# MoBA attention and a GELU MLP on one core: another ending for the last output tile, another gate in front of the weight loads, and a new order

## The chip, the cores and the metric

The kernel runs on one core of a Trainium2 chip. The metric is the device time of one execution in microseconds (us). Eleven runs of the kernel before gave a median of 259.63 us, from 258.48 to 269.83. The core's engines are called as in the profile: PE (matmuls; PEld is its weight load), DVE (vector), ACT (scalar), POOL (gpsimd), and SP, which does nothing here but issue DMAs.

## The reference

Four batches (B), eight heads, 768 tokens (S), head size 64. Attention is causal and block-sparse: a token sees its own block of 64 and the three blocks whose mean key scores highest with its query. Its output, 3072 tokens by 512, goes through an MLP with 2048 hidden units. Inputs and outputs are float32.

```python
k_rep = k.reshape(B, H, n_blocks, block, D).mean(axis=3)
gate_scores = np.einsum('bhsd,bhnd->bhsn', q, k_rep)     # causal blocks only
top_idx = np.argsort(gate_scores, axis=-1)[..., -top_k:] # 3 blocks, and the own one
scores = scale * np.matmul(q, k.transpose(0, 1, 3, 2))   # masked, causal
attn = softmax(scores); x = attn @ v                     # x: [3072, 512]
h = x @ w_in
g = 0.5 * h * (1.0 + np.tanh(c * (h + 0.044715 * h * h * h)))
out = g @ w_out
```

## The kernel before

**Work.** Heads are taken in 16 pairs `p`, four to a batch. `load` (L406) brings one of k, q, v of a pair from HBM with DMAs on SP: two for the plain form, four (one per half head and head) for the form that DVE then turns with a 32x32 stream transpose (L585). `pre` (L549) makes keys and queries with the head dimension on partitions, the block means, the gate and the selection (DVE, L709 to L730). `heads2` (batch 0, L847) and `heads` (batches 1 to 3, L1028) do scores (PE, L866 and L1049), exp (ACT, L885 and L1062), the causal triangle (POOL, L911 and L1076) and the product with v (PE, L934 and L1088). `s1` (L1114) is the first MLP product, 128 matmuls of 384 columns per batch (L1124) with the GELU on ACT (L1136) into `G`. `s2_plain` (L1200) is the second MLP product of batch 0, 96 matmuls of 512 columns (L1206). `s2` (L1241) does it for batches 1 to 3 with Strassen's scheme in Winograd's form: seven products of half size instead of eight. `sums` and `w_sums` make the factors on DVE (L1194, L1176).

**The Strassen tile.** `token(t)` (L1244) treats 128 rows of the upper half and 128 of the lower half of a batch together. `half(m, side, h, ...)` (L1248) is product `m`: eight matmuls of 256 columns (L1254) into one half `h` of a PSUM bank called `side`. Products run on PE strictly in the order of the calls, since each waits for `prev`. The order is 1, 5 (bank P), 2, 6 (bank Q), 3, 4 (P again), 7 (Q again). DVE or ACT copies product 1 to the output tile `osb` (`ao`), and DVE adds the rest in joins (L1298): `eo` makes product 5 + product 1, `bo`, `co` and `do` each add 512 columns. Product 3 waits for `eo`, and product 7 for `bo`, because they go on top of a bank that these joins read. After `co` and after `do` SP stores 128 rows of 512 float32 (256 KB each, L1331).

**Weights.** `load_w` (L476) issues a weight matrix in two parts of 1024 KB (as float16) on POOL's DMA queue. In front of the first part stands a small POOL copy (L482) that reads 16 numbers of a loaded tile, so that POOL does not issue the load before that tile has landed. For `w_in` the tile is that of v of pair 3; for `w_out` it is that of q of pair 4, of which the copy reads partition 0, which the first of its four DMAs writes. `hold` (L490) is a tiny DMA on SP that reads the first part of a weight; the loads behind it on SP wait until that part has landed: k and q of pair 4 stand behind `w_in`, v of pair 4 and everything later behind `w_out`.

**Order.** Everything is one list of `Op`s with dependencies, engine costs and a priority. `Plan.solve` (L200) is a list scheduler: at each step it takes, of the operations that could start first on their engines, the one with the lowest priority number. It works with the written costs (`{PE: 0.2215}`, `{"DMA": 6.0}`, `lag`), and its DMA resource is one first-come queue. The priorities are `RANK` (L21), 1881 numbers, one for each operation in the order of its creation. Each engine then runs its instructions in the order that came out, each waiting by semaphores for what it really needs. The numbers of `RANK` are thus the only thing that sets the order within an engine.

**Fillers.** `warm` (L1346) makes 72 matmuls of the identity (L1351) of the lowest priority. The scheduler puts one wherever it sees PE without other work. What is left over at the end runs after the last product, while the last store is on its way.

Of the kernel before, what the change touches and what calls it, by code (L numbers as in the profile page):

```python
# [21 lines left out]
    165, 130, 222, 240, 129, 241, 103, 211, 111, 84, 211, 61, 51, 212, 293,  # L22
    65, 212, 231, 42, 284, 32, 3, 284, 39, 4, 283, 49, 650, 1, 285, 121, 29,
    285, 71, 30, 284, 48, 394, 18, 286, 90, 26, 286, 110, 139, 285, 158,
    368, 138, 286, 60, 355, 28, 642, 624, 324, 73, 519, 522, 326, 105, 352,
    72, 99, 67, 1018, 377, 83, 496, 380, 82, 107, 24, 36, 76, 164, 162, 56,
    373, 91, 85, 81, 13, 89, 168, 86, 34, 190, 1029, 449, 971, 156, 102,
    100, 52, 381, 346, 75, 429, 416, 117, 118, 621, 313, 114, 113, 827, 298,
    514, 261, 178, 186, 384, 273, 188, 479, 361, 309, 134, 534, 271, 209,
    199, 396, 424, 198, 392, 189, 136, 115, 575, 214, 109, 140, 453, 142,  # L30
    756, 141, 494, 120, 639, 174, 232, 295, 233, 15, 163, 557, 35, 58, 557,
    43, 351, 300, 428, 300, 19, 171, 135, 148, 239, 315, 254, 101, 108, 526,
    378, 362, 314, 206, 490, 182, 552, 379, 180, 296, 451, 312, 512, 345,
    289, 548, 311, 169, 393, 318, 194, 74, 170, 365, 316, 339, 181, 172,
    383, 317, 395, 237, 63, 504, 319, 275, 382, 260, 729, 247, 290, 421,
    288, 643, 272, 353, 277, 281, 55, 448, 246, 320, 347, 524, 610, 208,
    195, 244, 503, 616, 521, 226, 310, 336, 1098, 390, 341, 364, 333, 573,
    155, 269, 299, 358, 323, 482, 527, 553, 321, 488, 425, 253, 200, 335,
    350, 363, 297, 294, 680, 1271, 1270, 388, 54, 98, 322, 668, 264, 343,
    78, 325, 203, 95, 359, 354, 786, 357, 789, 520, 434, 509, 342, 467, 437,  # L40
    790, 389, 93, 782, 435, 44, 334, 258, 469, 80, 565, 344, 399, 77, 413,
    837, 414, 94, 41, 557, 251, 259, 149, 774, 776, 775, 797, 582, 64, 1439,
    1003, 550, 933, 934, 794, 11, 38, 125, 502, 505, 619, 1019, 529, 66,
    263, 577, 431, 433, 709, 221, 474, 498, 407, 412, 470, 397, 452, 436,
    473, 307, 947, 608, 723, 1233, 147, 1332, 1342, 945, 1313, 625, 948,
    843, 841, 928, 144, 736, 759, 611, 765, 478, 764, 713, 766, 936, 438,
    688, 955, 670, 737, 724, 653, 967, 1034, 1442, 252, 654, 1090, 607, 833,
    193, 951, 862, 950, 1310, 532, 823, 769, 1275, 1013, 97, 493, 1111, 536,
    444, 992, 531, 644, 618, 578, 215, 712, 663, 767, 783, 822, 1016, 798,
    1267, 924, 1491, 1512, 1408, 1407, 689, 844, 1216, 8, 213, 1200, 958,  # L50
    838, 940, 1091, 944, 969, 792, 793, 282, 265, 242, 305, 587, 651, 655,
    507, 419, 561, 703, 705, 728, 640, 959, 960, 785, 1070, 1184, 1182,
    1249, 201, 204, 205, 248, 262, 104, 249, 677, 686, 697, 719, 707, 661,
    750, 385, 386, 622, 540, 544, 546, 492, 614, 491, 338, 374, 268, 303,
    515, 517, 617, 612, 631, 635, 641, 460, 443, 463, 462, 458, 456, 555,
    687, 1017, 835, 1187, 267, 500, 143, 202, 183, 176, 349, 450, 486, 487,
    735, 747, 748, 1163, 1160, 1541, 572, 483, 1208, 440, 441, 484, 331,
    411, 806, 814, 706, 191, 497, 511, 855, 585, 468, 648, 851, 746, 623,
    613, 1062, 14, 235, 600, 682, 1064, 784, 132, 153, 1183, 849, 131, 700,
    666, 229, 696, 306, 791, 404, 472, 558, 45, 695, 558, 23, 606, 558, 53,  # L60
    694, 228, 37, 57, 40, 423, 238, 420, 699, 308, 541, 398, 400, 1066, 12,
    79, 250, 157, 197, 123, 658, 681, 207, 154, 725, 704, 702, 243, 768,
    543, 302, 664, 173, 757, 698, 701, 236, 669, 376, 678, 96, 636, 568,
    372, 406, 518, 586, 538, 192, 559, 27, 391, 559, 33, 216, 559, 47, 758,
    22, 21, 882, 150, 223, 220, 224, 665, 369, 913, 909, 230, 660, 124, 270,
    62, 175, 601, 119, 234, 405, 567, 50, 445, 551, 615, 432, 861, 638, 69,
    489, 889, 799, 426, 632, 566, 159, 459, 634, 562, 278, 554, 570, 1068,
    605, 749, 480, 917, 304, 560, 46, 161, 560, 31, 255, 560, 25, 225, 196,
    122, 771, 772, 166, 184, 167, 513, 218, 337, 872, 874, 633, 70, 564,
    177, 301, 455, 563, 466, 684, 457, 1079, 576, 753, 446, 811, 464, 942,  # L70
    584, 754, 877, 1734, 348, 581, 807, 910, 447, 943, 1311, 179, 360, 371,
    692, 547, 744, 340, 593, 592, 387, 595, 1540, 780, 185, 755, 859, 580,
    495, 481, 740, 287, 367, 210, 579, 596, 628, 589, 501, 442, 1222, 1225,
    1304, 824, 817, 809, 921, 1026, 925, 603, 927, 962, 1377, 961, 996, 781,
    1086, 1320, 923, 868, 860, 926, 691, 1354, 330, 329, 773, 1110, 1143,
    994, 998, 1317, 717, 734, 821, 836, 1380, 1083, 1085, 1103, 1134, 1256,
    597, 796, 667, 718, 1274, 328, 332, 733, 815, 953, 898, 869, 974, 1294,
    1132, 883, 919, 1159, 1539, 1228, 1231, 1567, 952, 1072, 1157, 939,
    1234, 1232, 499, 409, 410, 731, 832, 972, 1717, 1105, 1106, 1578, 1643,
    1664, 1683, 732, 770, 1658, 1728, 1727, 1648, 1645, 1253, 1735, 1492,  # L80
    803, 1287, 1358, 1494, 1631, 1646, 1603, 1661, 1653, 858, 1640, 1715,
    1718, 1714, 886, 187, 356, 16, 1639, 847, 1171, 716, 714, 863, 675, 676,
    829, 867, 1028, 1048, 1080, 893, 894, 891, 887, 941, 761, 1047, 1137,
    1056, 1206, 1331, 1333, 1336, 1052, 762, 1381, 1379, 1378, 1454, 1099,
    1337, 620, 5, 1375, 935, 984, 1081, 1084, 1089, 1189, 1082, 1154, 1053,
    1168, 599, 1076, 476, 475, 528, 604, 477, 1051, 1421, 1322, 1343, 1374,
    970, 1403, 1361, 1447, 1071, 1515, 1520, 1365, 1584, 1104, 116, 227, 20,
    133, 890, 1738, 127, 890, 1742, 92, 890, 1749, 465, 375, 68, 146, 145,
    1009, 1069, 523, 598, 1015, 1199, 506, 1197, 657, 739, 1224, 471, 266,
    1308, 1542, 1186, 1156, 918, 1535, 1528, 916, 1245, 1627, 1666, 826,  # L90
    1142, 1329, 760, 1152, 1012, 1366, 1607, 1153, 530, 1041, 1543, 1282,
    549, 973, 1513, 831, 1219, 880, 978, 1357, 1000, 106, 892, 1741, 257,
    892, 1736, 126, 892, 1737, 788, 590, 370, 777, 778, 1097, 854, 545, 583,
    556, 1223, 1094, 1095, 418, 741, 804, 805, 864, 1496, 1511, 1155, 1014,
    1630, 1536, 1061, 1005, 1716, 1626, 1131, 1007, 1656, 991, 1531, 1642,
    1006, 673, 1522, 1063, 1024, 674, 1655, 1411, 1151, 846, 875, 292, 920,
    1165, 1135, 1301, 510, 895, 1748, 662, 895, 1733, 571, 895, 1750, 1725,
    1207, 439, 1675, 1676, 1205, 659, 485, 937, 1312, 1353, 1214, 1591, 276,
    742, 876, 871, 693, 1266, 881, 828, 1409, 884, 1025, 911, 914, 1055,
    1045, 839, 904, 1376, 1010, 1044, 813, 902, 1373, 853, 800, 1410, 908,  # L100
    845, 1399, 915, 1074, 1011, 626, 965, 1243, 820, 1020, 245, 896, 1744,
    88, 896, 1739, 763, 896, 1686, 1446, 1246, 1299, 1315, 1316, 1300, 1075,
    1302, 1732, 852, 857, 327, 1254, 217, 743, 993, 1021, 679, 1633, 1042,
    1367, 810, 1278, 1073, 1178, 866, 1321, 1067, 1326, 801, 1166, 1118,
    1078, 1037, 1453, 525, 1077, 1038, 1196, 602, 1280, 1150, 1050, 981,
    1284, 968, 1400, 1594, 1319, 537, 726, 1437, 1436, 1033, 1261, 656, 897,
    819, 976, 1001, 899, 906, 929, 999, 903, 722, 721, 720, 975, 963, 1696,
    1684, 1705, 1721, 1123, 1124, 1065, 1140, 1369, 1167, 1209, 1176, 1175,
    1713, 1251, 997, 995, 1255, 1711, 1148, 1088, 985, 1161, 1710, 1194,
    1114, 1726, 1036, 1141, 1059, 1096, 1147, 1722, 1144, 1113, 1146, 1172,  # L110
    1709, 1174, 1139, 1138, 1252, 1712, 1297, 1277, 1305, 1328, 1707, 1035,
    1745, 988, 990, 1002, 1115, 949, 1125, 1370, 1330, 1335, 1334, 1339,
# [69 lines left out]
class Plan:  # L182
# [12 lines left out]
    def add(self, *a, **kw):  # L195
        op = Op(*a, **kw)
        self.ops.append(op)
        return op
# [81 lines left out]
def kernel(  # L280
# [9 lines left out]
    nc = tc.nc  # L290
# [950 lines left out]
    def s2(b):  # L1241
# [95 lines left out]
        for t in range(NC // 2):  # L1337
            token(t)
# [107 lines left out]
```

## Time and profile before

| what | number |
|---|---|
| median of 11 runs, and the lowest | 259.63 us, 258.48 us |
| the profiled execution's own time | 259.15 us |
| its span (first to last instruction) | 257.4 us |
| busy: PE, DVE, ACT, POOL | 251.4, 179.3, 162.8, 86.2 us |
| PE: L1124, all L1254, L1206 | 512, 504 and 96 matmuls |
| granted PE clock | full speed in all 40 slices |
| DMA queues | 32.63 MB; eight tenths busy or more in nearly all slices until 135 us, then falling |

The profiled execution's time is 1.75 us more than its span; that is what lies around the instructions. A line of a group reads: source line, engine, operation, written tile and read tiles, shape, count, then busy time, mean time of one in ns, and the idle time before them with what ended it. In the chain of waits and the timeline the first two numbers are the start, in us from the start of the span, and the length. A matmul's length contains the time to run through the array, so neighbouring matmuls overlap: eight of 256 columns last 1.04 us, but the next eight start 0.87 us after them.

### The profile page before, as it was taken

What the parts mean: (1) busy time and instruction counts of PE and PEld (TensorE: products, weight loads), DVE (VectorE), ACT (ScalarE), POOL (GpSimd) and SP (SyncE); (2) the same over time, 40 slices, a digit from 0 to 9 for tenths busy, and PEclk for the clock granted to TensorE, in tenths of its full rate; (3) what the DMA queues carried; (4) which work ended last, traced back from release to release, by engine and by line L of the source; (5) the groups of instructions that cost most, each with busy time, mean ns of one, the idle gap of its engine ahead of it and who ended that gap; (6) DMA issues with size and microseconds to landing.
All of it is one profiled execution on the core that took longest, in us unless ns stands there. A gap on an engine that the chain in (4) does not pass through costs nothing.

```text
span 257.4 us, 6482 instructions
## 1 busy us (share of the span) xinstructions
PE 251.4 (98%) x2530; PEld 175.1 (68%) x2530; DVE 179.3 (70%) x525; ACT 162.8 (63%) x204; POOL 86.2 (33%) x168
## 2 busy tenths in 40 slices
PE   6999999999999999999999999999999999999996
PEld 5777776555455566555778787556777896657885
DVE  1887865031899999999999999997854452308542
ACT  2279678646678995667798397565888843664000
POOL 8755734011465575404153744010143310000000
PEclk9999999999999999999999999999999999999999
DMA  7999998999988989999994693312021132000222
GB/s 159 220 155 201 160 210 115 206 196 174 184 176 178 188 152 170 192 191 181 162 179 110 124 220 82 107 28 51 1 84 33 41 104 83 3 0 0 84 82 84
DMA packets 133951, 32.63 MB, mean 127 GB/s; under 512 B 127680, under 2 KB 129824, under 8 KB 133920
## 3 DMA queue, kind: packets, MB, share of 16 engines
q1 hardware_dynamic: 129184, 27.62, 53.8%
q0 software_dynamic: 3136, 4.19, 9.8%
q10 hardware_dynamic: 1600, 0.39, 0.7%
q8 instruction: 20, 0.33, 0.5%
q14 instruction: 11, 0.09, 0.1%
HBM read 27.26 MB, written 6.29 MB: 130 GB/s over the span
## 4 chain that ended last, share of the span: by engine, by line
PE 84%; DVE 12%; issue 1%; ACT 1%; POOL 0%; DVEq 0%; POOLq 0%
PE wide L1124 33%; PE bank L1254 18%; PE wide L1049 8%; PE bank L1206 6%; PE bank L1088 4%; PE wide L866 3%; PE bank L1351 3%; PE bank L693 2%; PE bank L934 2%; PE bank L566 2%; DVE qT L395 2%; DVE sel L725 1%; DVE osb L1298 1%; PE bank L991 1%; PE bank L762 1%
## 5 line engine op out<-in xcount | busy, mean ns | idle before, releaser
L1124 PE MATMUL wide<-xT,w_in 128*128 128x384 f16 x512 | 87.3, 326 | 0.0
L1136 ACT ACTIVATE G<-wide 128x768 f16<-128x768 f32 x64 | 51.8, 811 | 42.3 <-PE wide L1124 41.7
L1124 PEld LDWEIGHTS <-w_in 128*128 128x128 f16 x512 | 49.5, 98 | 33.0 <-issue 1.3
L1062 ACT ACTIVATE at<-wide 128x896 f16<-128x896 f32 x72 | 62.4, 916 | 12.5 <-PE wide L1049 10.4
L1076 POOL TENSOR_SCALAR_AFFINE_SELECT at<-at 128x256 f16<-128x256 f16 x72 | 31.5, 438 | 60.0 <-ACT at L1062 59.2
L1049 PE MATMUL wide<-qT,kT 76*128 76x512 f16 (+3 forms) x192 | 38.2, 305 | 0.3 <-DVE qT L395 0.3
L393 POOL CAST kT<-k 64x768 f16<-64x768 f32 x20 | 17.3, 870 | 43.8 <-DVE k L585 42.9
L1254 PEld LDWEIGHTS <-G 128*128 128x128 f16 x288 | 27.1, 97 | 5.2 <-issue 0.5
L1254 PE MATMUL bank<-w_out,G 128*128 128x256 f16 x216 | 30.1, 272 | 0.3 <-DVE osb L1298 0.3
L1298 DVE TENSOR_TENSOR osb<-bank,osb 128x512 f32<-128x512 f32 (+1 forms) x36 | 22.2, 618 | 11.0 <-PE bank L1254 10.8
L1206 PE MATMUL bank<-w_out,G 128*128 128x512 f16 x96 | 27.0, 379 | 0.0
L1088 PEld LDWEIGHTS <-at 128*128 128x128 f16 x504 | 21.9, 98 | 4.1
L1049 PEld LDWEIGHTS <-kT 76*128 76x128 f16 x192 | 17.1, 98 | 10.5 <-issue 1.1
L885 ACT ACTIVATE at<-wide 128x1024 f16<-128x1024 f32 (+3 forms) x24 | 20.8, 917 | 4.8 <-PE wide L866 4.7
L1088 PE MATMUL bank<-v,at 128*128 128x65 f16 x504 | 23.8, 194 | 0.0
L1254 PEld LDWEIGHTS <-XS 128*128 128x128 f16 x216 | 20.3, 98 | 3.1 <-DVE zr L971 0.3
L1254 PE MATMUL bank<-TS,XS 128*128 128x256 f16 x144 | 20.8, 272 | 0.0
L585 DVE STREAM_TRANSPOSE k<-ksd 128x768 f32<-128x768 f32 x12 | 11.5, 967 | 10.3 <-DMA ksd<-in_k_dram 10.3
L1194 DVE TENSOR_TENSOR XS<-G 128x768 f16<-128x768 f16 x12 | 7.2, 604 | 16.1 <-ACT G L1136 15.9
L1351 PE MATMUL bank<-ident 128*128 128x256 f16 x72 | 12.9, 302 | 2.3 <-DVE ident L323 2.3
L972 DVE TENSOR_TENSOR xn<-bank,zr 128x384 f16<-128x384 f32 x24 | 13.4, 558 | 0.8
L725 DVE MAX8 sel<-sel 128x8 f32<-128x12 f32 x160 | 13.2, 157 | 0.6
(97 smaller groups left out, 316.2 us busy)
## 6 DMA issues: line engine op xcount, KB each, us to landing
out_dram<-osb SPq DMA_DIRECT2D x24, 256.0 KB, 2.6
vsd<-in_v_dram SPq DMA_DIRECT2D x26, 192.0 KB, 3.8
qsd<-in_q_dram SPq DMA_DIRECT2D x48, 96.0 KB, 2.7
ksd<-in_k_dram SPq DMA_DIRECT2D x48, 96.0 KB, 3.2
w_in<-in_moe_w_in_dram POOLq DMA_DIRECT2D x2, 1024.0 KB, 10.8
w_out<-in_moe_w_out_dram POOLq DMA_DIRECT2D x2, 1024.0 KB, 13.6
G<-in_k_dram SPq DMA_DIRECT2D x4, 192.0 KB
G<-in_v_dram SPq DMA_DIRECT2D x4, 192.0 KB, 4.8
```

The lines of the kernel that those rows point to most:

```text
L393: nc.gpsimd.tensor_copy(out=out, in_=in_)
L885: nc.scalar.activation(out=T["at", u][:, :, 0:n], in_=plan.buf[("st",) + u].rearrange("p (h w) -> p h w", h=2)[:, :, 0:n], func=AF.Exp, bi ...
L1049: nc.tensor.matmul(st[:, x:e], kT16[i][h][0:76, s0:s0 + 128], qT16[i][h][0:76, s0 + (x - cb):s0 + (e - cb)], start=True, stop=True)
L1062: nc.scalar.activation(out=T["at", u][:, 0:n], in_=plan.buf[("st",) + u][:, 0:n], func=AF.Exp, bias=0.0, scale=SCALE)
L1076: nc.gpsimd.affine_select(out=dg, in_=dg, compare_op=ALU.is_ge, fill=0.0, base=0, pattern=[[0, 2], [1, 128]], channel_multiplier=-1)
L1088: nc.tensor.matmul(pvv[:, qc, 0:65], at[:, cb + (qc - jc) * 128: cb + (qc - jc + 1) * 128], v16[i][:, jc, h, :], start=(gi == 0 and jc == ...
L1124: nc.tensor.matmul(hps[:, 512 * e:512 * e + HALF], w_in16[:, ci, (2 * j + e) * 128: (2 * j + e + 1) * 128], T["xT", b][:, ci, HALF * h:HAL ...
L1136: nc.scalar.activation(out=G[:, :, h, j, :], in_=plan.buf["hps", b, j, h].rearrange("p (e w) -> p e w", e=2)[:, :, 0:HALF], func=AF.Gelu_a ...
L1206: nc.tensor.matmul(plan.buf["ops", b, ti], G[:, f % 2, 2 * ti // NC, f // 2, ti % (NC // 2) * 128:ti % (NC // 2) * 128 + 128], w_out16[:, ...
L1254: nc.tensor.matmul(dst[:, HD * h:HD * h + HD], FACT[m][0][:, j, t * 128:(t + 1) * 128], FACT[m][1][:, j, :], start=(clear and j == 0), sto ...
L1298: nc.vector.tensor_tensor(out=dst(), in0=src(), in1=other(), op=ALU.add)
L1351: nc.tensor.matmul(plan.buf["warm", n][:, 0:256], ident16, z, start=True, stop=True)
```

## The change

Three edits, in the words of the code:

1. `load` remembers the tile of the load issued last (`T["latest"]`). The gate of a weight load reads that tile instead of a named one, and in two places, so that it waits for the first and the last of the load's DMAs. The plan's dependencies follow: `w_in` after v of all four pairs of batch 0 instead of v of pair 3, `w_out` after k and q of pair 4 instead of q alone.
2. The last tile of the last batch goes through a new function, `ending`. Product 2 comes last and has a bank of its own (R). There are seven small DVE steps, and three stores instead of two: the upper half row in two halves of 256 columns (128 KB each, SP), the lower half row whole (256 KB, on ACT's queue).
3. `RANK` is another list throughout. It has three numbers more (1884), because `ending` has three operations more. The fillers have the last rank in both.

```diff
 RANK = [
-    165, 130, 222, 240, 129, 241, 103, 211, 111, 84, 211, 61, 51, 212, 293,
...
+    205, 206, 219, 362, 204, 310, 74, 213, 103, 91, 213, 84, 150, 217, 421,
...
@@ load, in emit and in emit_t
-            T[key, p] = sd
+            T[key, p] = T["latest"] = sd
@@ load_w
             if after is not None:
                 x = const.tile([1, 16], FP32, name=f"after_{name}")
-                nc.gpsimd.tensor_copy(out=x, in_=T[after][0:1, 0, 0, 0:16]
-                                      if len(T[after].shape) == 4 else
-                                      T[after][0:1, 0, 0:16])
+                y = T["latest"]
+                for n, z in ((0, y[0:1, 0]), (8, y[96:97, y.shape[1] - 1])):
+                    if len(y.shape) == 4:
+                        z = z[:, n // 8]
+                    nc.gpsimd.tensor_copy(out=x[:, n:n + 8], in_=z[:, 0:8])
             nc.gpsimd.dma_start(out=dst[part], in_=view[part])
@@ token
+            if b == B - 1 and t == NC // 2 - 1:
+                return ending(half, quad, two, bank_of, a_e, join, key, post)
@@ s2
+        def ending(half, quad, two, bank_of, a_e, join, key, post):
+            def store(deps, h, n0, n1, eng):
+                def emit(_):
+                    (nc.sync if eng == SP else nc.scalar).dma_start(
+                        out=out_rows[key[0] * NC + key[1] + NC // 2 * h][
+                            :, HD * n0:HD * n1],
+                        in_=T["osb", key][:, h, n0:n1].rearrange(
+                            "p n d -> p (n d)"))
+                add({eng: 0.55}, emit, deps, -50, lag=2.2)
...
+            half(1, "P", 1, True, [])
+            mm = half(5, "P", 0, False, [])
...
+            ao = add({DVE: 0.45, ACT: 0.45}, a0_e, [mm], post,
+                     takes=("osb", ("osb", key)))
+            eo = add({DVE: 0.34}, join(
+                lambda: quad(3), of("P", 0), lambda: quad(0)), [ao], post)
+            mm = half(6, "Q", 1, True, [])
+            bo = add({DVE: 0.34}, join(
+                lambda: quad(1), of("Q", 1), lambda: quad(0)), [mm, ao], post)
+            half(3, "P", 0, False, [eo])
+            mm = half(4, "P", 1, True, [])
+            go = add({DVE: 0.34}, join(
+                lambda: quad(2), of("P", 1), lambda: quad(0)), [mm], post)
+            co = add({DVE: 0.34}, join(
+                lambda: quad(1), of("P", 0), lambda: quad(1)), [mm, bo], post,
+                gives=[])
...
+            store([co], 0, 1, 2, SP)
+            mm = half(7, "Q", 1, False, [bo])
+            do = add({DVE: 0.66}, join(
+                lambda: quad(2, 2),
+                lambda: two(bank_of("Q")[:, HD:2 * HD]).to_broadcast(
+                    [128, 2, HD]),
+                lambda: quad(2, 2)), [mm, go, eo], post)
+            store([do], 1, 0, 2, ACT)
+            mm = half(2, "R", 0, True, [])
+            last_op = add({DVE: 0.34}, join(
+                lambda: quad(0), of("R", 0), lambda: quad(0)), [mm, do], post)
+            store([last_op], 0, 0, 1, SP)
@@ the calls of load_w, for w_in and w_out
-            [ld["v", 3]], -200 + x, None if x else ("v", 3))
+            [ld["v", x] for x in range(HP)], -200 + x, None if x else "v")
...
-            [ld["q", HP]], 40, None if x else ("q", HP))
+            [ld["k", HP], ld["q", HP]], 40, None if x else "q")
```

Where the two lists put a few operations (a number of `RANK`, lower goes first among what is ready):

| operations | before | after |
|---|---|---|
| issue of k and of q of pair 4 | 163, 58 | 399, 501 |
| the 64 steps (two matmuls each) of `s1` of batch 0, L1124 | 397 to 1442 | 42 to 1200, 50 of them below 1051 |
| the first nine steps of `s2_plain`, L1206 | 663 to 1267, three of them below 770 | 1051 to 1130 |

## The prediction

> **What bounds the kernel now.** I read the page first, then the busy times by stretch, the chain of waits, and the timelines of SP, POOL, DVE and PE around the places that the change touches. The cut at 39.1 us is the first matmul of the MLP (L1124), the one at 253.28 the end of the last product.
>
> ```profile
> span 257.4 us, 6482 instructions
> PE 251.4 (98%) x2530; PEld 175.1 (68%) x2530; DVE 179.3 (70%) x525; ACT 162.8 (63%) x204; POOL 86.2 (33%) x168
> ```
>
> ```profile
> 0.00:39.10 39.10, 35.98 (x524) 27.29 (x525) 26.36 (x116) 23.78 (x31) 24.59 (x60) 1.00 1.03 184
> 39.10:253.28 214.18, 213.51 (x1993) 146.35 (x1991) 152.22 (x408) 138.98 (x174) 61.57 (x109) 1.00 0.59 116
> 253.28:257.40 4.12, 1.96 (x18) 1.51 (x16) 0.69 (x1) 0.00 (x0) 0.00 (x0) 1.00 0.33 127
> ```
>
> After each stretch's length stand the busy times of PE, PEld, DVE, ACT and POOL. PE is the bound: in 214.2 us of the middle it is idle 0.67. But "busy" includes fillers and overlapping ends, so I count the work by its steps. The chain's pieces give the time of one:
>
> ```profile
> 97.29 1.51 PE bank L1206 x7
> 99.56 0.43 PE bank L1088 x14
> 104.31 8.88 PE wide L1124 x54
> ...
> 182.38 0.38 PE wide L1049 x3
> ...
> 236.46 16.81 PE bank L1254 x154
> ```
>
> L1124: 512 x 0.1644 = 84.2 us. L1254: 504 x 0.1092 = 55.0. L1206: 96 x 0.2157 = 20.7. Scores L1049: 72 units (the 72 exps of L1062) x 0.38 = 27.4. L1088: 36 x 0.43 = 15.5. Twelve gates L693 at 0.41 (chain) = 4.9. Transposes and what is left of pair 3 make 3.9. Sum 211.6. So of 214.2 us only **2.6 us** are not work; nine fillers of 0.11 are about 0.8 of it, waits the rest. No order can win more than that there. In the first 39.1 us PE idles 3.1 and has 9.6 us under fillers. About 5.2 of the two pass before the first key has landed (the chain's first L566 is at 5.45), so some 7.5 us are open to an order in principle. What ends last in that stretch is the attention of pairs 0 to 3, a ladder through PE, DVE, ACT and POOL.
>
> **Part 1, the gate of the weight loads.** The place where chip and plan part:
>
> ```profile
> 40.02 2.29 SPq L427 DMA_DIRECT2D ksd<-in_k_dram  x4
> ...
> 52.15 0.57 SPq L493 DMA_DIRECT2D held_out<-w_out  x1
> ```
>
> ```profile
> 40.49 0.19 POOL L482 COPY after_out<-qsd 1x16 f32<-1x16 f32 x1
> 40.63 1.78 POOL L485 DMA_DIRECT2D w_out<-in_moe_w_out_dram x2
> ```
>
> ```profile
> 55.54 0.98 DVE L585 STREAM_TRANSPOSE k<-ksd 128x768 f32<-128x768 f32 x1 [10.26 <-DMA ksd<-in_k_dram]
> ```
>
> The gate sees the first DMA of q at 40.49 and lets 2048 KB of `w_out` go while k of the same pair is being issued. That k load takes 13.8 us, where the median row of ksd is 3.2, and DVE stands 10.26 us for it. In the changed kernel the gate opens when the last DMA of both has landed. Issue ends at 42.3, plus 1.2 for the later `w_in` (below), plus 2.7 to 3.2 to land: 46.2 to 46.7. So k is there 9 us earlier, and `w_out` goes at about 46.8, 6.2 later. Its first part landed 11.5 us after its issue with k beside it; `w_in`'s took 9.4. Thus 56.2 instead of 52.1 by the latter (58.3 by the former), the second part about 5 later.
>
> Removed: DVE's wait. The k chain behind it (L585 0.98, L628 0.95, half a cast 0.54, L645 0.18: 2.65 us of DVE) moves into the hole, out of the stretch 55 to 180, in which DVE is busy 113 of 125 us (17.85 and 95.19 in two windows) and where the chain of waits runs through DVE from 66.4 to 76.0. Since PE was fed from L1206 meanwhile, this is not worth 10 us, nor 2.65, but at most the 2.6 us that PE loses in the middle. Lower end 0 (the waits stay), upper 2.6. I take half, **-1.3**, as the idle rows of PE (0.33 in 55 to 80, 0.34 in 80 to 180) lie evenly inside and behind that stretch.
>
> Added: `w_out` 4 us later, and with it everything on SP behind `held_out`. The next loads have this room: k of pair 5 is issued until 58.6, lands 3.2 later at 61.8, is used at 65.55, so 3.7; q of pair 5 4.7, pair 6 over 5. A shift of 4 costs 0 to 0.3. L1206 itself must wait for 56.2 instead of starting at 53.57; the new list puts 50 of the 64 L1124 steps in front of it, 50 x 0.33 us from 39.3 plus about 1 us of other work, so PE asks at about 56.7. Cost 0 (hidden by L1124), up to 1.6 at 58.3.
>
> The gate of `w_in`: the copy ran at 25.13 before; the load issued last (SP, 23.13 to 24.22; landing 2.9 by its row) is complete at about 26.7. POOL stands 1.5 us longer. Behind it in POOL's queue stand the cast of q of pair 3 (26.83, which waited for DVE till then), the cast of v, and the triangle at 29.11; they move by about 1.2, which the 1.03 us of idle POOL before 30.55 nearly absorbs. PE ran fillers at 30.54 and 31.19, so there is no cover if one of them is late: 0 to +1.2. I take 0, since `w_in` landed at 34.7 (25.26 + 9.4) for a use at 39.3, and the new order may place the casts otherwise. SP's `held_in` moves from 34.7 to about 36, the 1.2 used above. The second copy is 0.19 on an engine that is idle two thirds of the time.
>
> [...]
>
> **Part 2, the ending.**
>
> ```profile
> 248.75 1.04 PE L1254 MATMUL bank<-w_out,G 128*128 128x256 f16 x8
> ...
> 252.24 1.04 PE L1254 MATMUL bank<-w_out,G 128*128 128x256 f16 x8
> 253.11 2.13 PE L1351 MATMUL bank<-ident 128*128 128x256 f16 x18
> ```
>
> ```profile
> 248.95 0.42 DVE L395 COPY osb<-bank 128x256 f32<-128x256 f32 x1 [1.05 <-PE bank L1254]
> 249.41 0.42 DVE L1298 TENSOR_TENSOR osb<-bank,osb 128x256 f32<-128x256 f32 x1
> ...
> 253.31 0.69 DVE L1298 TENSOR_TENSOR osb<-bank,osb 128x512 f32<-128x512 f32 x1 [0.18 <-PE bank L1254]
> ```
>
> The seven products are the same work. But product 2 (248.75) stood between 5 and 3 and covered `eo`, which ends at 249.83. Now only product 6 does, until 249.62. PE waits till about 249.89, 0.27 us, or 0.38 if a filler gets in the way. Product 7 then starts at 251.64 and 2 at 252.51; the last result is out at 253.55, not 253.28. On DVE: `go` and `co` until 252.72, `do` 252.76 to 253.45, the last join 253.59 to 254.01. The last store is issued at 254.04; before, at 254.03 (253.31 + 0.69 and a step). So the shorter last join (0.42 for 0.69) only pays for the new stall. What is left is the smaller store: 256 KB moved in 0.70 us (the rows of DMA by stretch show 337 GB/s from 254.95 to 255.65 and nothing after). Half the bytes take 0.35 to 0.70, as the rows become 1 KB. `do`'s store, issued 0.55 earlier on ACT, is through by then, 0.9 us after its issue plus 0.7. Gain 0 to 0.35; I take **-0.3**. Ends: -0.5 and +0.4 (two stores collide, a filler more).
>
> The second queue brings nothing: an issue on SP is 0.33 us, and SP would be free at 253.8. [...]
>
> **Part 3, the order.** It touches everything and shows in no row. Its bounds are those of part 1: up to 2.6 us in the middle, in the first stretch 7.5 at the far end. The nearest row is the old order itself, which filled the middle to 99%. I take 0 beyond part 1.
>
> **Sum.** -1.3 - 0.3 = -1.6 on the profiled execution: 259.15 - 1.6 = 257.55, of it 255.8 span and 1.75 around. That execution is 0.48 under the median; on the median of 259.63 the forecast is **258.0 us**. About 0.5%, 1.3 us, is what a measurement of this kernel can tell from no change.
>
> **Rivals.** (a) *PE was fed anyway.* For it: 0.67 us idle in 214, and L1206 covers every DVE delay. Then only the ending counts, 259.3; with POOL's gate late by 1.2, 260.5. Within 0.5%. (b) *PE meets `w_out` too early.* PE runs in order, and the plan takes 6.0 + 1.6 us for a part's landing (`load_w`), against rows of 9.4 and 11.5. If L1206 stands where the plan expects it, PE halts before it near 57 us, with no filler. Each us of landing behind 56.7 costs one: 1.6 by 11.5 us, and 2.4 more if the last load of pair 4 takes the 5.1 of qsd's slowest. Price 1.6 to 4.0, say 2.6, the middle's gain lost: 261.9. It turns the sign once `w_out` lands behind 58.6. Against it: the ranks of L1206. (c) *The new list is better than its bounds in part 3 suggest*, filling a third of the first stretch's 7.5 us: 255.5.
>
> **Chances.** Forecast 0.42, with its own range 256.5 to 258.3; (a) 0.34; (b) 0.19; (c) 0.05. Faster 0.47, same 0.34, slower 0.19. The range goes from 256.2 to 261.4: at the low end tail and middle at their bounds, at the high end the cheaper half of (b).
>
> **What would show it.** Right: the gate copy reads the tile at 46 to 47 us; DVE's k transpose of pair 4 starts before 48 without a wait of us; ksd's longest landing falls below 6; PE's idle and fillers between 39 and 253 fall from 2.6 to about 1.3; the last store is issued within 0.1 us of where the sum puts it, and one filler or a 0.3 us gap stands in front of product 3. Wrong: a gap of PE in front of the first L1206; DVE waits for ksd of pair 5; the first L1124 moves from 39.1 by more than 1 us either way, which would make the order, not the gate, the cause.

## The result and the profile after

The kernel after the change takes **262.01 us** (median of 12 runs, 261.12 to 262.67) beside 259.5 us for the kernel before on the same chip: a ratio of 1.0095, with a 95% interval of 1.0076 to 1.0115. It is slower by 2.5 us, where 258.0 was predicted, and 0.6 us above the upper end of the range. The profiled execution took 261.71 us, with a span of 260.0. All ratios here leave out the slow executions of a kernel, such as those near 269 us of the kernel before, and the differences in us are worked out from the ratios.

The page and the busy times by stretch, cut at the same three places as before: the first MLP matmul (39.25 us) and the end of the last product (256.47). After each stretch's length stand the busy times of PE, PEld, DVE, ACT and POOL.

```profile
span 260.0 us, 6488 instructions
...
PE 252.1 (97%) x2530; PEld 174.0 (67%) x2530; DVE 178.2 (69%) x524; ACT 167.4 (64%) x208; POOL 88.1 (34%) x169
```

```profile
0.00:39.25 39.25, 35.78 (x512) 25.96 (x513) 25.74 (x114) 23.95 (x30) 25.22 (x61) 1.00 0.89 160
39.25:256.47 217.22, 216.29 (x2022) 148.06 (x2018) 152.01 (x409) 143.47 (x178) 62.85 (x108) 1.00 0.60 119
256.47:260.00 3.53, 0.00 (x0) 0.00 (x0) 0.42 (x1) 0.00 (x0) 0.00 (x0) 1.00 0.39 141
```

The first stretch is 0.15 us longer, the middle 3.0, the end 0.6 shorter. In the middle PE still looks full (idle 0.93 of 217.2), because the scheduler's fillers stand in its holes. To see past them I count PE by its work: each matmul but a filler gets the usual time from its start to the next start, and what is left of the clock time is "lost", be it a wait, a filler or a slow stretch. All kernels below do the same 236.0 us of work by this count. Each row is one profiled execution; those of runs 7 and 10 (gate of `w_in` alone; three loads not held) took 0.9 us more than their medians, and that of run 8 (gate of `w_out` alone) 1.5 less.

| lost PE time, us, by stretch of each kernel's own time | 0 to 30 | 30 to 46 | 46 to 65 | 65 to 100 | 100 to 125 | 125 to 253 | all |
|---|---|---|---|---|---|---|---|
| before | 11.51 | 2.17 | 0.13 | 1.46 | 0.13 | 1.82 | 17.22 |
| after | 10.69 | 4.78 | 0.12 | 0.77 | 2.28 | 1.74 | 20.38 |
| old order, both new gates | 11.74 | 3.24 | 4.23 | 1.37 | 0.23 | 1.86 | 22.67 |
| old order, new gate of `w_in` alone | 11.85 | 4.92 | -0.05 | 1.40 | 0.14 | 1.91 | 20.17 |
| old order, new gate of `w_out` alone | 11.63 | 2.21 | 1.27 | 1.55 | -0.03 | 1.90 | 18.53 |
| new list and ending, old gates | 10.81 | 3.52 | 0.12 | 0.69 | 2.52 | 1.74 | 19.40 |
| the same, three loads not held | 11.01 | 3.65 | 0.60 | 0.67 | 2.55 | 1.80 | 20.28 |

So the change loses 2.6 us more between 30 and 46 us and 2.2 more between 100 and 125, and gains 0.7 between 65 and 100. (The first column also holds when the first inputs landed; the same instructions lost 11.5 to 12.7 there in different kernels of the old order. So differences below 1 us in it, such as the 0.8 here, are not read.)

**30 to 46 us.** POOL in the kernel after, around the two gates:

```profile
27.82 0.42 POOL L486 COPY after_in<-vsd 1x8 f32<-1x8 f32 x2
30.36 1.67 POOL L487 DMA_DIRECT2D w_in<-in_moe_w_in_dram  x2 [2.12 <-issue]
```

```profile
48.35 0.18 POOL L486 COPY after_out<-qsd 1x8 f32<-1x8 f32 x1
48.79 0.18 POOL L486 COPY after_out<-qsd 1x8 f32<-1x8 f32 x1 [0.26 <-DMA qsd<-in_q_dram]
49.24 1.78 POOL L487 DMA_DIRECT2D w_out<-in_moe_w_out_dram  x2 [0.27 <-issue]
```

The `w_in` load goes at 30.36 instead of 25.26: its gate copies run 2.7 us later than the one of before, and then POOL stands 2.12 us for nothing that the profile shows. The triangle behind it on POOL is late for PE, and the second part of `w_in` lands at 44.39, which is where the chain of waits of after runs:

```profile
33.31 0.24 PE L936 MATMUL bank<-v,at 128*128 128x65 f16 x2 [0.99 <-POOL at L913]
```

```profile
31.27 13.12 DMA w_in<-in_moe_w_in_dram
44.45 7.97 PE wide L1126 x48
52.83 6.61 PE wide L1126 x40
59.44 0.43 PE bank L1208 x2
```

Between 42.5 and 44.2 us PE has eight fillers. Then 88 matmuls of the first MLP product come, with only one gate of 0.41 us among them, and the first L1208 (L1206 before) starts when `w_out` has just landed (58.98).

**46 to 100 us.** This is where the gain was to come from. DVE in the kernel after, and below it one row of the kernel before that the prediction passed over:

```profile
46.04 0.98 DVE L587 STREAM_TRANSPOSE k<-ksd 128x768 f32<-128x768 f32 x1 [1.59 <-DMA ksd<-in_k_dram]
...
64.73 0.49 DVE L395 COPY qT<-bank 12x640 f16<-12x640 f16 x1 [9.68 <-PE bank L764]
68.05 0.98 DVE L587 STREAM_TRANSPOSE k<-ksd 128x768 f32<-128x768 f32 x1 [2.83 <-DMA ksd<-in_k_dram]
```

```profile
63.47 0.35 DVE L709 STREAM_TRANSPOSE sel<-bank 128x160 f32<-128x160 f32 x1 [5.40 <-PE bank L693]
```

The transpose of k of pair 4 is at 46.04 instead of 55.54, and its wait is 1.59 instead of 10.26. But the idle time has not gone: DVE now waits 9.68 us for PE (L764, the transposes of the mask), which in PE's order stand at 64.25. And in the kernel before, the next wait of DVE behind the 10.26 us is already one for PE, of 5.40 us. The k chain had that much slack. The wait of 2.83 us for k of pair 5 is one of the prediction's signs of being wrong. It comes from the later loads, but PE loses less between 65 and 100 us than before, and run 10, which takes the wait away, is no faster than the kernel it is made from.

**100 to 125 us.** PE in the kernel after, and then in the kernel before, where the first matmuls of batch 1 are mixed with other work:

```profile
103.76 0.60 PE L1403 MATMUL bank<-ident 128*128 128x256 f16 x4
104.20 0.50 PE L993 MATMUL bank<-ident,xn 128*128 128x128 f16 x6
104.53 0.60 PE L1403 MATMUL bank<-ident 128*128 128x256 f16 x4
104.97 0.81 PE L1126 MATMUL wide<-xT,w_in 128*128 128x384 f16 x4
```

```profile
100.37 0.81 PE L1206 MATMUL bank<-w_out,G 128*128 128x512 f16 x3
101.02 0.50 PE L991 MATMUL bank<-ident,xn 128*128 128x128 f16 x6
101.36 0.81 PE L1124 MATMUL wide<-xT,w_in 128*128 128x384 f16 x4
102.01 0.59 PE L1206 MATMUL bank<-w_out,G 128*128 128x512 f16 x2
```

L1403 is the filler. In the same places the old list has matmuls of the second MLP product of batch 0. The new list has run the last of them by 101.5 us; the old one keeps two until 120.59.

**The ending**, PE and then DVE in the kernel after:

```profile
250.80 1.91 PE L1256 MATMUL bank<-TS,XS 128*128 128x256 f16 x16
252.81 1.03 PE L1256 MATMUL bank<-w_out,XS 128*128 128x256 f16 x8
253.68 1.04 PE L1256 MATMUL bank<-TS,G 128*128 128x256 f16 x8
254.56 1.91 PE L1256 MATMUL bank<-w_out,G 128*128 128x256 f16 x16
```

```profile
256.50 0.42 DVE L1300 TENSOR_TENSOR osb<-bank,osb 128x256 f32<-128x256 f32 x1 [0.18 <-PE bank L1256]
```

The step before 252.81 is 0.26 us too long, that is `eo`; the last join is 0.42 us instead of 0.69, and the last store is through 3.53 us after the last product instead of 4.12.

### The profile page after: what moved, and what is told of

Its sections match the earlier page's. It is cut to its first block, busy times and chain, and to the rows that moved or that the text cites. A ratio compares the mean times of both kernels' runs of the same rounds, so it can differ in the third digit from the quotient of the medians.

```text
span 260.0 us, 6488 instructions
## 1 busy us (share of the span) xinstructions
PE 252.1 (97%) x2530; PEld 174.0 (67%) x2530; DVE 178.2 (69%) x524; ACT 167.4 (64%) x208; POOL 88.1 (34%) x169
## 4 chain that ended last, share of the span: by engine, by line
PE 76%; DVE 10%; DMA 7%; issue 2%; POOL 2%; ACT 1%; DVEq 0%; SPq 0%; POOLq 0%; ACTq 0%
PE wide L1126 23%; PE bank L1256 21%; PE wide L1051 10%; PE bank L1208 6%; PE bank L1090 6%; DMA w_in<-in_moe_w_in_dram 5%; PE bank L1403 2%; PE bank L695 2%; PE wide L868 2%; PE bank L568 1%; DVE k L587 1%; DMA qsd<-in_q_dram 1%; DMA mT<-madd 1%; DVE ks L630 1%; DVE qT L395 1%
## 5 line engine op out<-in xcount | busy, mean ns | idle before, releaser
L1126 PE MATMUL wide<-xT,w_in 128*128 128x384 f16 x512 | 88.2, 326 | 0.1
L1126 PEld LDWEIGHTS <-w_in 128*128 128x128 f16 x512 | 48.8, 98 | 32.2 <-issue 1.3
L1064 ACT ACTIVATE at<-wide 128x896 f16<-128x896 f32 x72 | 63.1, 917 | 9.5 <-PE wide L1051 7.8
L1078 POOL TENSOR_SCALAR_AFFINE_SELECT at<-at 128x256 f16<-128x256 f16 x72 | 33.3, 465 | 62.9 <-ACT at L1064 62.5
L1051 PE MATMUL wide<-qT,kT 76*128 76x512 f16 (+3 forms) x192 | 38.9, 305 | 0.1
L1208 PE MATMUL bank<-w_out,G 128*128 128x512 f16 x96 | 26.5, 379 | 0.0
L393 POOL CAST kT<-k 64x768 f16<-64x768 f32 x19 | 16.7, 881 | 26.7 <-DVE k L587 26.2
L393 POOL CAST v<-vsd 128x768 f16<-128x768 f32 x13 | 11.7, 907 | 17.6 <-DMA vsd<-in_v_dram 17.5
L1403 PE MATMUL bank<-ident 128*128 128x256 f16 x72 | 13.5, 301 | 2.3 <-DVE ident L323 2.3
L587 DVE STREAM_TRANSPOSE k<-ksd 128x768 f32<-128x768 f32 x12 | 11.5, 967 | 4.5 <-DMA ksd<-in_k_dram 4.4
```

What stands on the lines that cost most here:

```text
L393: nc.gpsimd.tensor_copy(out=out, in_=in_)
L1051: nc.tensor.matmul(st[:, x:e], kT16[i][h][0:76, s0:s0 + 128], qT16[i][h][0:76, s0 + (x - cb):s0 + (e - cb)], start=True, stop=True)
L1064: nc.scalar.activation(out=T["at", u][:, 0:n], in_=plan.buf[("st",) + u][:, 0:n], func=AF.Exp, bias=0.0, scale=SCALE)
L1078: nc.gpsimd.affine_select(out=dg, in_=dg, compare_op=ALU.is_ge, fill=0.0, base=0, pattern=[[0, 2], [1, 128]], channel_multiplier=-1)
L1126: nc.tensor.matmul(hps[:, 512 * e:512 * e + HALF], w_in16[:, ci, (2 * j + e) * 128: (2 * j + e + 1) * 128], T["xT", b][:, ci, HALF * h:HAL ...
L1208: nc.tensor.matmul(plan.buf["ops", b, ti], G[:, f % 2, 2 * ti // NC, f // 2, ti % (NC // 2) * 128:ti % (NC // 2) * 128 + 128], w_out16[:, ...
```

## The experiments

The time of every kernel stands beside runs of the kernel before on the same chip. Theory G: the gates cost the time. Theory O: the new list does. In the texts on record the theory of the list is called L for runs 1 to 4; for runs 9 and 10 L is the late loads and O the order.

**1. Old list, old ending, both new gates.** The plan's dependencies stay too, so that every engine has the order of before; only the copies differ.

```diff
-                nc.gpsimd.tensor_copy(out=x, in_=T[after][0:1, 0, 0, 0:16]
+                y = T["latest"]
+                for n, z in ((0, y[0:1, 0]), (8, y[96:97, y.shape[1] - 1])):
...
+                    nc.gpsimd.tensor_copy(out=x[:, n:n + 8], in_=z[:, 0:8])
```

> The old list and the old ending; only the small POOL copies in front of the weight loads are the new ones, so every engine keeps its old order. Theory G (the gates: weights that go later push the whole load chain on SP back, and PE runs out of work): slower, 260.5 to 261.5; first w_out part issued at about 46.5 instead of 40.6 us, held_out 4 to 6 us later, PE's lost time after 100 us grows by over 1 us. Theory L (the list itself is the worse one, the gates are harmless): 259.5 within 0.5, and the 10.3 us wait of DVE for k of pair 4 is gone.

Measured: 264.56 us, 1.019 [1.0148, 1.0233]: 4.9 us slower, more than either theory expected. PE, then POOL:

```profile
57.24 0.59 PE L1213 MATMUL bank<-w_out,G 128*128 128x512 f16 x2 [2.34 <-DMA w_out<-in_moe_w_out_dram]
```

```profile
44.43 0.18 POOL L487 COPY after_out<-ksd 1x8 f32<-1x8 f32 x1 [2.63 <-DMA ksd<-in_k_dram]
46.41 0.24 POOL L487 COPY after_out<-ksd 1x8 f32<-1x8 f32 x1 [1.80 <-DMA ksd<-in_k_dram]
46.87 1.78 POOL L492 DMA_DIRECT2D w_out<-in_moe_w_out_dram  x2 [0.21 <-issue]
```

The gate does what it says: no k load takes more than 3.9 us (13.8 before). But PE halts 2.34 us in front of `w_out`, and soon after runs at a lower clock (0.50 for 3.41 us, last section), so 4.2 us go between 46 and 65. DVE's 10.26 us for k turn into one wait for PE:

```profile
68.98 0.35 DVE L716 STREAM_TRANSPOSE sel<-bank 128x160 f32<-128x160 f32 x1 [19.19 <-PE bank L700]
```

From 65 to 125 us this kernel loses 1.60 us of PE, the kernel before 1.59. DVE's wait was worth nothing.

**2. The ending alone**, with the old list (ranks for its three further operations made up so that the rest keeps its order) and the old gates.

```diff
+            if b == B - 1 and t == NC // 2 - 1:
+                return ending(half, quad, two, bank_of, a_e, join, key, post)
...
+    ranks = RANK[:1772] + [0] * 39 + RANK[1808:]
```

> The old list and the old gates; only the last tile goes through the new ending. Both theories: the ending is good, 259.2 (-0.3, from -0.5 to 0): a hole of 0.27 us or two fillers in front of product 3, and 0.6 us less from the last product's end to the span's end. If the loss were in the ending, this would be 260 or more.

Measured: 259.27 us, 0.9999 [0.9971, 1.0028]. No difference that can be measured.

**3. The kernel after with `w_in` issued early**, without its gate, ahead of the cast of q on POOL.

```diff
-            [ld["v", x] for x in range(HP)], -200 + x, None if x else "v")
+            [ld["v", x] for x in range(HP)], -200 + x, None)
...
+    at = next(n for n, op in enumerate(order) if op is plan.ops[129])
+    order[at:at] = lws
```

> The changed kernel with both w_in loads moved ahead of two casts on POOL and without their gate copies; all else in the new order. Theory G: w_in is issued at about 26.4 instead of 30.4 us, PE no longer waits for POOL at 33 nor for the second part at 44 (together 2.3 us), and the loads behind held_in come 4 us earlier, which gives back part of the loss at 100 to 125: 258.5 to 260. Theory L: only PE's wait for POOL goes, 261 to 261.5.

Measured: 262.81 us, 1.0154 [1.011, 1.0198]. The load goes at 26.38 and there is no gap on POOL, but 30 to 46 us still lose 4.20 (after 4.78), the 2.07 between 100 and 125 stay, and a wait of 1.7 us for the transposed x (a DMA) appears that ends at 161.39. The expected gain did not come, so the load's time alone does not set these stretches. But the test is not clean: the casts that the load now precedes go later (that of q at 28.02 us instead of 26.33).

**4. The kernel after with `w_out` issued early**, at 41.57 us, without its gate.

```diff
-            [ld["k", HP], ld["q", HP]], 40, None if x else "q")
+            [ld["k", HP], ld["q", HP]], 40, None)
...
+    at = next(n for n, op in enumerate(order) if op is plan.ops[304])
+    order[at:at] = lws
```

> The changed kernel with both w_out loads moved ahead of the cast of k of pair 4 on POOL and without their gate copies; all else in the new order. Theory G: w_out is issued at about 41 instead of 49.2 us, held_out 6 to 8 us earlier, the loads behind it too, and the loss of 2.2 us between 100 and 125 goes: 259.8 to 260.5, with a longer landing of k and q of pair 4. Theory L: 262 within 0.5, as the fillers at 102 to 107 stand where the list put them and the work that L1208 did before them is used up.

Measured: 273.47 us, 1.0567 [1.0515, 1.0619]. SP's issues, then DVE's and PE's waits (in total, times, longest):

```profile
45.64 13.08 SPq L427 DMA_DIRECT2D qsd<-in_q_dram  x4
```

```profile
DVE k L587 <- DMA ksd<-in_k_dram: 12.8, 1, 12.8
```

```profile
PE bank L695 <- DVE ksb L647: 8.4, 1, 8.4
```

This is 14.7 us over the kernel before, where the two theories expected 262.5 us in all at most. A weight load beside k and q costs 8.4 us of PE here (and the mean granted clock of the execution is 0.985, by my estimate 271.4 x 0.015 = 4 us more over the span), and nothing in the kernel before, where the clock is 1.00, though DVE waits about as long in both (12.8 and 10.26 us). The difference is PE's order: the new list asks for the gate of pair 4 (L695) near 52 us, the old one at 62.92 (L693). The new list needs a gate there; run 6 shows that the old one will do.

**5. The kernel after without the fillers planned behind 39 us.**

```diff
+    order = [op for op in order if op.start < 39 or op.eng != PE
+             or "warm" not in op.emit.__qualname__]
```

> The changed kernel without the 24 fillers that the new list puts behind 39 us (8 at 41 to 44, 16 at 100 to 107); they compute nothing that is used. Theory F (fillers run in program order, so each costs its slot of 0.109 us even where PE has work by then): 24 x 0.109 = 2.6 us less, 259.4. Theory G (PE has nothing to do there, because the weight loads and the loads behind them are late): 261.5 to 262.

Measured: 262.26 us, 1.0095 [1.0066, 1.0124], as with them. Where they stood, PE now shows what it waits for:

```profile
105.24 0.81 PE L1126 MATMUL wide<-xT,w_in 128*128 128x384 f16 x4 [0.24 <-ACT xT L391]
106.62 1.46 PE L1126 MATMUL wide<-xT,w_in 128*128 128x384 f16 x8 [0.57 <-ACT G L1138]
```

**6. The new list and ending with the old gates**, every engine in the order of after.

```diff
-                y = T["latest"]
...
+                nc.gpsimd.tensor_copy(out=x, in_=T[after][0:1, 0, 0, 0:16]
```

> The changed kernel with the old gates, in the plan too: w_in after v of pair 3, w_out after the first DMA of q of pair 4. The order that the list gives stays the same on every engine, as in this list v of pair 3 and q of pair 4 are the loads issued last anyway. All theories: 262 within 0.5, since POOL reaches both gates behind casts that open no earlier. Should it be below 261, the second copy of the gate costs by itself (for one the 2.1 us in which POOL stands between the copies and the w_in DMA).

Measured: 261.0 us, 1.0061 [1.0035, 1.0086], where 261.5 to 262.5 was expected. So the list (with the ending) costs 1.6 us by itself. The gates cost about 0.9 more on top: the executions of the kernel after and of this one differ by 0.96 us (95% interval 0.5 to 1.4), the spans are 259.1 and 260.0, and 3.52 against 4.78 us are lost from 30 to 46. `w_in` goes at 28.07 here, with no gap behind the copy. The run also shows that the new list does not need the new gate for k of pair 4. DVE, then POOL:

```profile
44.52 0.98 DVE L585 STREAM_TRANSPOSE k<-ksd 128x768 f32<-128x768 f32 x1 [0.94 <-DMA ksd<-in_k_dram]
```

```profile
46.96 1.95 POOL L485 DMA_DIRECT2D w_out<-in_moe_w_out_dram  x2
```

This list issues k ahead of q (ranks 399 and 501, before 163 and 58), so that the old gate, which reads q, opens when k has landed.

**7 and 8. One new gate at a time in the old order.**

```diff
-                nc.gpsimd.tensor_copy(out=x, in_=T[after][0:1, 0, 0, 0:16]
+                if after in ['v']:
+                    y = T["latest"]
...
+                else:
+                    nc.gpsimd.tensor_copy(out=x, in_=T[after][0:1, 0, 0, 0:16]
```

(`['q']` in the other.)

> The old kernel and order with the new gate in front of w_in alone. Theory G: about 1 us of the 5.1 that both gates cost: w_in 2.3 us later, POOL blocked and PE late by 1 us at 30 to 35; then w_out, which has the old gate, goes about 1 us later: 260.3 to 261.2. If the gate of w_in is harmless: 259.5.

> The old kernel and order with the new gate in front of w_out alone. Theory G in the form of rival (b) of the prediction (PE in order meets L1206 before w_out has landed): w_out issued at about 45.5 us, its first part there at about 56, PE stands 2 us or more at 55 to 60 in front of L1206, and the rest comes from the loads behind held_out: 262.5 to 263.8. If the gate of w_out is harmless or good, as the prediction had it: 258.2 to 259.5.

Measured: 261.19 us, 1.0058 [1.0026, 1.0089], for `w_in`, and 261.93 us, 1.0082 [1.0048, 1.0116], for `w_out`. The first is as theory G had it; the second lies between its two expectations. In its profile PE waits 1.11 us for `w_out`, less than expected, because `w_in` and so `held_in` and pair 4 come earlier than in run 1 (`w_out` issued at 44.83, in run 1 at 46.87). That execution took 260.41 us, 1.5 less than the median, so the profile shows only part of the 2.1 us. Together the gates cost more (4.9) than the sum of the two (3.6); the lower clock behind the halt of run 1, 1.7 us, is enough for the rest. The gate of `w_in` showed something else: DVE, and POOL beside it.

```profile
30.61 3.35 DVE L723 TENSOR_TENSOR sel<-sel,cgate 128x120 f32<-128x120 f32 x1
```

```profile
30.92 0.84 POOL L393 CAST v<-vsd 128x768 f16<-128x768 f32 x1
31.69 1.00 POOL L918 TENSOR_SCALAR_AFFINE_SELECT at<-at 128x256 f16<-128x256 f16 x2
32.64 0.82 POOL L393 CAST v<-TS 128x768 f16<-128x768 f32 x1
33.42 1.03 POOL L918 TENSOR_SCALAR_AFFINE_SELECT at<-at 128x256 f16<-128x256 f16 x2
```

This addition usually takes 0.28 us (the median of 17 in the kernel before). Here it lasts from 30.61 to 33.95 while POOL, late behind its gate, works off what has piled up without a gap, and PE waits 2.74 us for the mask that is made from it.

**9. The kernel before with only the later loads late**: the hold for `w_out` reads the weight's second part.

```diff
-            nc.sync.dma_start(out=x, in_=src[0:1, 0, 0:16])
+            n = src.shape[1] // 2 if name == "out" else 0
+            nc.sync.dma_start(out=x, in_=src[0:1, n, 0:16])
```

> The kernel before, unchanged but that the hold for w_out on SP reads the second part of the weight and not the first: v of pair 4 and every later load are issued when the second part has landed (57.15 us in the trace of before) and not the first (52.15), 5 us later, about the shift that the change brings them (6.85). Nothing else moves. Theory L (the change loses its 2.2 us between 80 and 125 us because these loads are late): PE loses 1.5 to 2.5 us more than before in that stretch, and the time is 261 to 262 us. Rival O (the order itself, which has used up the L1206 steps by 100 us): the loads' room of 3.7 to 5 us takes the shift up, PE loses at most 0.4 us more, and the time is 259.4 to 260.0.

Measured: 259.5 us, 1.0008 [0.9982, 1.0034]. The hold went at 57.72 instead of 52.15, and it cost nothing that can be measured.

**10. Run 6 with three loads not held.**

```diff
+    order.remove(held[1])
+    at = max(order.index(op) for op in free)
+    order.insert(at + 1, held[1])
```

> The new list with the gates of before (261.0 us, L1206's last steps gone by 100 us, 2.5 us of PE lost between 100 and 125), and on SP the hold for w_out stands behind v of pair 4 and k and q of pair 5 and no longer ahead of them: these three loads go from about 45 us and not from 57.2. They share the DMA engines with w_out, which I expect to land 1 to 3 us later (58 to 60 for its first part; PE asks for it near 58). Theory L (late loads cause the loss between 100 and 125): that loss falls by 1 us or more, and the time is 259.2 to 260.4. Rival O (the order itself): the loss there stays at 2 to 2.5 us and the time is 261.0, up to 262.5 if w_out lands behind the point where PE asks.

Measured: 260.71 us, 1.0047 [1.0022, 1.0071]. DVE has k of pair 5 without a wait:

```profile
65.05 0.98 DVE L585 STREAM_TRANSPOSE k<-ksd 128x768 f32<-128x768 f32 x1
```

Still 2.55 us are lost between 100 and 125 (run 6: 2.52). With run 9 this excludes the late loads, and run 5 the fillers. What is left is the list, which has no work for PE there; no run put such work back.

**11. Run 7 with POOL waiting for DVE's addition**: one copy of eight numbers, ahead of the two casts and the triangles.

```diff
+                if p == 3:
+                    after_add = const.tile([1, 8], FP32, name="after_add")
+                    nc.gpsimd.tensor_copy(out=after_add,
+                                          in_=T["gm", p][0:1, lo, 0, 0:8])
```

> The old order with the new gate on w_in alone (261.2 us), in whose profile one DVE addition of the selection of pair 3 (128x120 float32, two inputs in SBUF) takes 3.35 us where its median is 0.27, while POOL runs two casts and three triangles without a gap; PE then waits 2.7 us for madd. Added: one copy of 8 numbers on POOL, which reads the result of that addition and stands ahead of those casts, so that POOL lets the addition through; POOL's order is otherwise the same. Theory P (POOL without a gap keeps DVE out): the addition takes under 0.6 us, PE's longest wait for madd falls below 1.2 us, and the time is 259.6 to 260.6, although a wait was added. Rival G (POOL is late behind the gate, and what depends on its casts and triangles is late whatever DVE does): PE still loses 2 us or more between 30 and 40 us, and the time is 261.0 to 261.8.

Measured: 261.96 us, 1.0099 [1.0064, 1.0133], not faster than run 7. DVE, then POOL:

```profile
31.32 0.28 DVE L723 TENSOR_TENSOR sel<-sel,cgate 128x120 f32<-128x120 f32 x1
```

```profile
31.66 0.18 POOL L730 COPY after_add<-sel 1x8 f32<-1x8 f32 x1 [0.58 <-DVE sel L723]
```

The addition takes 0.28 us again, PE's longest wait for the mask is 0.6 us, and 30 to 46 us lose 2.65 instead of 4.92. So the profile is as theory P had it, but its expected time was missed. Part of the gain is lost again behind it: by the same count about 0.9 us more than in run 7 go between 100 and 125, where PE waits 0.71 us for a DMA (`xT`), and the spans are 260.3 and 260.0. And POOL without a gap is not enough to keep DVE out so long: in run 1, where POOL works off the same casts and triangles without a gap from 30.08 to 33.69, the same addition is short.

```profile
30.50 0.56 DVE L723 TENSOR_TENSOR sel<-sel,cgate 128x120 f32<-128x120 f32 x1
```

The profiled execution of run 7 took 262.05, 0.9 over its median; how often the addition is kept out so long in other executions the runs don't show, and why run 11 is no faster stays open.

## Why the prediction was wrong

- *PE is the bound and 2.6 us are not work*: right in kind, if a little low; the table has 3.5 us between 46 and 253. That there was little to win in the middle was the safest number in it.
- *The gate of `w_out` frees k of pair 4*: it does in the old order (ksd 13.8 to 3.9 in run 1), and the transpose stands at 46.04, "before 48"; but in the new list the order does it already (44.52 with the old gate, run 6). **The step that failed first is the one that priced it: "I take half, -1.3".** Its worth is 0: 1.60 against 1.59 us lost behind it in run 1. The row that says so was in the trace of before, eight us after the wait: DVE's next wait is for PE, 5.40 us. The bound of PE's 2.6 us was an upper end without a mechanism, and half of it was no estimate.
- *"Cost 0 (hidden by L1124)"* for the later `w_out`: right for the new list (PE asks at 59.27; landed 58.98), and 2.34 us plus the clock in the old order. The shift of the later loads, *"0 to 0.3"*: right (run 9: 0).
- *POOL 1.5 us longer, "I take 0"*: mis-sized. `w_in` went 5.1 us later and not 1.5, and the last copy of the gate of `w_out` read its tile at 48.79 and not at 46 to 47. In the profile PE waits 1.0 us for a triangle behind it. Both gates together cost about 0.9 us in the new list (run 6), that of `w_in` 1.5 in the old order (run 7).
- *The ending, -0.3*: the parts came out as worked out (0.26 for 0.27; the tail 0.6 shorter), and the runs cannot tell the sum from 0.
- *The order, "0 beyond part 1"*: **the largest of the terms that failed.** The list costs 1.6 us (run 6). My bounds allowed only gains; a list that uses its later work early also leaves PE without any later, 2.4 us from 100 to 125.
- *Rival (b)*, the slower side: its sign and nearly its time came true (it said 261.9), but not its place: PE does not halt before L1208 in the kernel after. It does in runs 1 and 8, the old order. I read the ranks rightly, and the new list avoids that halt by putting 88 first-product matmuls in front, and pays for it elsewhere.

By its parts: -1.6 was forecast and +2.5 measured, 4.1 us apart. Of these 1.3 and 0.3 are the gains that did not come, 1.6 is the list with the ending, and 0.9 the gates. In the old order the gates alone cost 4.9. What stays open is why the list loses 1.35 us more than the old one between 30 and 46 us with the old gates (3.52 against 2.17), and the 2.12 us of POOL before the `w_in` load. In run 5, with the same POOL order, it was 1.03, so it is no fixed cost of the two copies.

Of the versions tried none beats the kernel before; the ending alone and run 9 equal it.

## What to carry to other kernels

Before a wait is priced as a gain, look at the next wait of the same engine: if that is for the bound engine, the time may be slack, and removing it only renames it, as with the 10.26 us here. A gate that delayed a transfer here delayed what stood behind it on its engine and on SP's queue (PE waited 0.99 us for the triangle behind the gate of `w_in`; the loads behind `w_out` went 5.1 us later in run 1), so price such a gate at the place where the bound engine asks for the last link in its own order. And a new order is not free by default: ask which spare work it uses early, and what covers the stretch that this work covered before.

## What the hardware showed unexpectedly

**The clock after a halt.** In run 1 PE is at full clock until it halts for 2.34 us. The busy times by stretch of that kernel, with the granted clock behind the five engines:

```profile
54.90:57.24 2.34, 0.00 (x0) 0.00 (x0) 0.00 (x0) 0.52 (x1) 0.00 (x0) 1.00 1.10 152
57.24:57.97 0.73, 0.73 (x4) 0.38 (x4) 0.00 (x0) 0.00 (x0) 0.00 (x0) 1.00 1.25 209
57.97:61.38 3.41, 3.41 (x12) 1.52 (x10) 0.00 (x0) 0.00 (x0) 0.00 (x0) 0.50 1.23 218
61.38:65.00 3.62, 3.62 (x23) 2.06 (x21) 0.00 (x0) 2.20 (x3) 0.83 (x1) 1.00 0.90 159
```

From 0.73 us behind the halt 3.41 us pass at half the clock, 3.41 x 0.50 = 1.7 us more: a halt of 2.3 cost about 4.0. The executions of run 1 fit this: five of the six have a mean clock of 0.993 or 0.994 and take 263.27 to 265.58 us, the one at 1.00 takes 262.55. In run 7 the clock stayed at 1.00 after 2.74 us in the profiled execution, and two of its twelve have 0.993. So the length of the halt alone does not decide it; what else does was not shown.

**A DVE addition 3 us late beside POOL.** In run 7 the addition takes 3.35 us where its median is 0.28. It ended about 3 us late, behind two casts and three triangles of POOL in a row, although its recorded start is 0.31 us ahead of the first cast. That POOL kept it out is read from this one execution and from run 11, where POOL waits and the addition takes 0.28 us. Run 1, where it takes 0.56 us with POOL at work on the same casts and triangles, shows that it need not happen. By what means POOL does it was not shown.
